# Four moves in a fused forward and backward transformer block: loads of x, constants, a layer norm's transposes, output gradients

## The chip, the cores and the metric

The kernel runs on one core of a Trainium2 chip. The metric is the device time of one execution in microseconds (us), lower is better. Every time quoted is from the runs of the kernel before, or from its profile, which is one profiled execution.

The engines are TensorE (PE, with PEld for its weight loads), VectorE (DVE), ScalarE (ACT), GpSimd (POOL) and SyncE (SP). Each takes its instructions in order. SP, ACT and POOL also issue transfers.

## The reference

One block on x of 2048 rows by 512 columns in bf16, forward and backward:

```
h  = x + attention(layernorm(x)) @ wo      # 32 heads of 16, each row sees 8 earlier rows, 2 apart
h2 = h + gelu(layernorm(h) @ w1 + b1) @ w2 + b2          # w1: 512 x 1792, w2: 1792 x 512
outputs: h2, and the gradients of x, wqkv, wo, w1, b1, w2, b2 for a given grad_out
```

The layer norms have no weights. The backward pass needs the normalised rows, attention's coefficients, q, k, v and the gelu's derivative.

## The kernel before, in words

The 2048 rows are cut into four chunks of 512. A tile of a chunk has 128 partitions; row-major tiles (`xt`, `ln1`, `ht`, `ln2`) hold four groups of 128 rows, feature-major tiles (`ln1T`, `ln2T`, `qt`, `kt`, `vt`) hold the transposes.

**Phase 1** is attention forward. Per chunk c:

- `p1_ln(c)` loads x into `xt` (L350, on SP's queue), normalises it on DVE (L194 statistics, L195, L198 `ve`, L199 `rstd` as a power on POOL, L201 `nm`, L203 four `ln` instructions), stores the rows by POOL's queue (L179), and transposes them on PE (L187) with copies on ACT (L188).
- `p1_qk(c)` and `p1_v(c)` are the projections (L366 on PE, L368 copies on ACT); `to_tm_store` (L235 on PE, L238 on ACT, L240 on SP) writes v, k and q back to memory row by row, through three staging buffers `tmst`.
- `p1_dots(c)` makes the products of q with eight shifted k's: four DVE instructions `pr` of 128x4096 (L257) and 64 small matmuls (L261). `p1_sm1`, `p1_sm2` are the softmax: maxima on DVE (L406, L410, L414) between copies on ACT (L404, L408, L412), a row-shift matmul (L416), exponentials (L419), sums (L427), reciprocal (L431), `attn` (L437).
- `p1_o(c, sc)`, twice per chunk, gathers rows of v by an indirect transfer from POOL's queue into one of two buffers `R` (L249), multiplies on DVE (`prb`, L287, four instructions) and sums on PE (`ps_band`, L292); `ost` is copied on ACT (L450), stored by POOL's queue (`o_d`, L453) and transposed into `oT` (L304, L305).
- `p1_d(c)` multiplies by wo and adds x (L463, L464, copy `h` L465), normalises h, stores it and transposes it into `ln2T[c]`.

`p1_round(c)` calls these for several chunks at once. The functions give an order of work and its dependencies; a scheduler then orders each engine's instructions up to the start of phase 3, so that an instruction may stand well ahead of or behind its place in the text.

**Before phase 1** stand the constants: `ident` (made on POOL), `Pmat`, `S32`, `Sum4`, `nSum4`, `Sm`, `ind8`, `Emat` (on DVE, L110 to L128), `mk` and the gather's row numbers `rowi` (on POOL, L130 to L145), and a few constant fills.

**SP's loads** take eight completion counters in turn. Where a load would take one that is in use, it waits for the transfer that used it last. Before: the x of chunk 0, three pieces of wqkv, four small stores of zeros (L476), `b1b` (L477), `b2row` (L478), then the x of chunks 1, 2 and 3. `b1b`, `b2row` and these three x loads wait for the first five transfers.

**Phase 2** is the MLP, forward and backward: projections `ps_h` (L577), gelu on DVE and ACT, `ps_f` (L609), `ps_gg` (L622), `ps_gl` (L633), with transposed loads and stores on SP (L561, L714 to L718).

**Phase 3** is attention backward. Here the order is written out by hand: `slot(us)` is called after each large DVE step, runs the PE work that was put off by `later(n, ...)` for n slots, and fills up with matmuls of the weight gradients (`filler`). `p3_go(c)` puts off four steps for chunk c: `a` transposes gh into `ghT`, `b(0)` and `b(2)` make two 128x512 groups each of `got = gh @ wo^T` (`go_mm`: L642 four matmuls, L643 a copy on ACT), `t` transposes and stores got. The tile `ps_go` is in the two-buffer pool psY, as `ps_band` (L1015) of the bands is. `psL` is a pool of one buffer of two banks that holds `ps_ga`. For chunk 1 all four steps run in one slot; chunk 0 is done earlier by `p3_pre`.

Of the kernel before, what the change touches and what calls it, by code (L numbers as in the profile page):

```python
# [10 lines left out]
P = 128  # L11
# [6 lines left out]
DH = 16  # L18
# [13 lines left out]
def _sub(apobj, dims, off=0):  # L32
    return _ap(apobj, [apobj.ap[0]] + [list(d) for d in dims], off)
# [3 lines left out]
def kernel(  # L37
# [29 lines left out]
    CH = 512  # L67
# [42 lines left out]
    V.tensor_copy(out=_sub(Pmat[:], [[1, 8], [8, DH]]), in_=_sub(ident[:], [[DH, 8], [1, DH]]))  # L110
    S32 = const.tile([P, 32], BF16, name="S32")
    for j in range(4):
        V.tensor_copy(out=S32[32 * j:32 * j + 32, :], in_=ident[32 * j:32 * j + 32, 32 * j:32 * j + 32])
    Sum4 = const.tile([P, P], BF16, name="Sum4")
    V.tensor_copy(out=Sum4[:].rearrange("p (a b) -> p a b", a=4), in_=S32[:].unsqueeze(1).to_broadcast([P, 4, 32]))
    nSum4 = const.tile([P, P], BF16, name="nSum4")
    V.tensor_scalar(out=nSum4[:], in0=Sum4[:], scalar1=-1.0, scalar2=None, op0=ALU.mult)
    Sm = const.tile([P, 4, P], BF16, name="Sm")
    V.memset(Sm[:], 0.0)
    for j in range(4):  # L120
        V.tensor_copy(out=Sm[32 * j:32 * j + 32, j, :], in_=Sum4[32 * j:32 * j + 32, :])
    ind8 = const.tile([P, 8], BF16, name="ind8")
    with nc.allow_low_precision(reason="exact 0/1 sums"):
        V.tensor_reduce(out=ind8[:], in_=ident[:].rearrange("p (a b) -> p a b", b=DH), axis=mybir.AxisListType.X, op=ALU.add)
    Emat = const.tile([P, 4, 32], BF16, name="Emat")
    V.memset(Emat[:], 0.0)
    for g in range(4):
        V.tensor_copy(out=Emat[:, g, 8 * g:8 * g + 8], in_=ind8[:])  # L128
    mk = const.tile([16, 2, 4, 32], BF16, name="mk")
    G.memset(mk[:], 0.0)  # L130
    for hf in range(2):
        G.affine_select(out=mk[:, hf], in_=mk[:, hf], compare_op=ALU.is_ge, fill=NEG, base=-2 * hf,
                        pattern=[[-4, 4], [0, 32]], channel_multiplier=1)
    ones_row = const.tile([1, P], BF16, name="ones_row")
    V.memset(ones_row[:], 1.0)
    ones_col = const.tile([P, 1], BF16, name="ones_col")
    V.memset(ones_col[:], 1.0)
    mhalf = const.tile([P, TPC], F32, name="mhalf")
    V.memset(mhalf[:], -0.5)
    zrow = const.tile([18, D], BF16, name="zrow")  # L140
    V.memset(zrow[:], 0.0)
    rowi = const.tile([P, 2], mybir.dt.uint32, name="rowi")
    for w4 in range(4):
        for b_, o in ((0, 4 * w4), (1, 4 * (3 - w4))):
            G.iota(rowi[32 * w4:32 * w4 + 32, b_:b_ + 1], pattern=[[0, 1]], base=o * D, channel_multiplier=8 * D)  # L145
# [201 lines left out]
    def p1_ln(c):  # L347
        xp, xg = ((wff, "w20"), (wff, "w28"), (early, "xt"), (late, "xt"))[c]
        xt = xp.tile([P, TPC, D], BF16, name="xt", tag=xg, bufs=1)
        load_rows(xt, xf, c)  # L350
        if c == 0:
            for i in range(3):
                o = (1, 0, 2)[i] * D
                SY.dma_start(out=wqkv[:, :, o:o + D], in_=A_wqkv[:, o:o + D].rearrange("(a p) j -> p a j", p=P))
        ln1 = early.tile([P, TPC, D], BF16, name="ln1", tag="ln1", bufs=2)
        layernorm(early, xt, rstd1, c, ln1)
        store_rows(ln1_d, c, ln1)
        ln1T = early.tile([P, DC, CH], BF16, name="ln1T", tag="ln1T", bufs=2)
        to_fm(ln1, ln1T)
        st_[c].update(xt=xt, ln1T=ln1T)  # L360
# [95 lines left out]
    def p1_d(c):  # L456
        d = st_[c]
        oT, xt = d["oT"], d["xt"]
        ht = htile(f"h{c}")
        for j in range(TPC):  # L460
            ps = X("ps_wo")
            for k in range(DC):
                T.matmul(ps[:], lhsT=oT[:, k, j * P:(j + 1) * P], rhs=wo[:, k, :], start=(k == 0), stop=False)  # L463
            T.matmul(ps[:], lhsT=ident[:], rhs=xt[:, j, :], start=False, stop=True)  # L464
            A.copy(out=ht[:, j, :], in_=ps[:])  # L465
        h_all.append(ht)
        ln2 = late.tile([P, TPC, D], BF16, name="ln2", tag="ln2", bufs=1)
        layernorm(late, ht, rstd2, c, ln2)
        store_rows(ln2_d, c, ln2)
        to_fm(ln2, ln2T[c])  # L470

    p1_ln(0)
    p1_qk(0)
    p1_dots(0)
    for (d_t, r) in ((v_d[0], 0), (k_d[0], 0), (q_d[NC - 1], CH), (go_d[NC - 1], CH)):
        SY.dma_start(out=d_t[r:r + RPAD, :], in_=zrow[:])  # L476
    SY.dma_start(out=b1b[:], in_=B_b1.rearrange("(f p) -> f p", p=P))  # L477
    SY.dma_start(out=b2row[:], in_=B_b2.rearrange("(a n) -> a n", a=1))  # L478
    G.dma_start(out=wo[:], in_=A_wo.rearrange("(a p) j -> p a j", p=P))
    p1_ln(1)  # L480
    p1_v(0)
# [6 lines left out]
    def p1_round(c):  # L488
        if c + 2 < NC:
            p1_ln(c + 2)  # L490
        if c + 1 < NC:
            p1_dots(c + 1)
        if c > 0:
            p1_d(c - 1)
        if c == NC - 2:
            p1_v(c + 1)
        if c + 2 < NC:
# [98 lines left out]
    def p2_rest(c):  # L596
# [33 lines left out]
        for j in range(TPC):  # L630
# [5 lines left out]
            ln_bwd(ffp["B"], ps[:], ln2[:, j, :], rstd2[:, t:t + 1], gout[:, j, :], gh[:, j, :])  # L636
            yield

    def go_mm(g, ghT, got):
# [3 lines left out]
        A.copy(out=got[:, g, :], in_=ps[:])  # L643
# [57 lines left out]
    p1_o(NC - 1, 1)  # L701
    run(hn, 1)
    p1_d(NC - 1)
    late.release()
    ffp["B"] = LP("ffB", "right")
    for k in range(SA, NS):
# [321 lines left out]
    def p3_go(c, at=(1, 2, 3, 4)):  # L1028
        ghT = pt3("ghT")
        got = pt3("got")  # L1030
        st3[c]["got"] = got

        def a():
            to_fm(gh_all[c], ghT)

        def b(g0):
            def f():
                for g in range(g0, g0 + 2):
                    go_mm(g, ghT, got)
# [185 lines left out]
```

## Time and profile before

| | us |
|---|---|
| median of 14 runs | 680.89 |
| lowest and highest run | 673.22 and 687.92 |
| the profiled execution's own time | 679.42 |
| its span in the profile | 677.5 |
| PE, DVE, ACT, POOL busy | 616.9, 512.9, 368.8, 150.2 |
| mean granted PE clock | 0.982 |

The profile's timeline gives start, duration, engine, line, output <- input, count, and in brackets how long the engine sat idle just before and what ended that. A chain of waits names who waited, for whom, how long in total, how often and the longest. A busy share is a mean over stages with different limits: PE is busy 80.32 of the first 100 us, 65.97 of the next 80, and 57.87 of the 60 after that.

### The profile page before, as it was taken

The numbers are of one execution on the slowest core, as the hardware profiler recorded it, in microseconds if no ns is written. First come the engines' busy times: TensorE is split into PE (matmuls) and PEld (weight loads), VectorE is DVE, ScalarE is ACT, GpSimd is POOL, SyncE is SP. The second block draws the span as 40 slices with busy tenths as digits, with TensorE's granted clock in tenths as the row PEclk, the third lists the DMA queues.
The fourth block names the chain that finished last, engine by engine and source line by source line (L and its number), as shares of the span: only waits on it lengthen the run. The fifth ranks groups of instructions, "written<-read, shape, count | busy, mean of one in ns | idle before, by whom it ended". The sixth has DMA issues, their size and how long they took to land. (4 is left out here: it accounts for less than half of the span.)

```text
span 677.5 us, 10267 instructions
## 1 busy us (share of the span) xinstructions
PE 616.9 (91%) x3948; PEld 289.4 (43%) x3948; DVE 512.9 (76%) x758; ACT 368.8 (54%) x576; POOL 150.2 (22%) x183
## 2 busy tenths in 40 slices
PE   3799998787999999999999898899989999988997
PEld 1343443333444344444344433434456576433443
DVE  6789989689779869869839697877977898296400
ACT  1497887699583555645440542763485357363311
POOL 4141635423001110110100251210322124030100
PEclk9999999988899999999999998999989999999999
DMA  7482959635999978978977899774898589969141
GB/s 256 153 293 88 299 191 306 209 133 125 231 208 282 245 199 193 233 226 186 228 236 186 288 349 379 263 272 171 289 402 309 189 278 340 326 236 317 62 155 47
DMA packets 147806, 158.87 MB, mean 235 GB/s; under 512 B 94461, under 2 KB 132398, under 8 KB 141102
## 3 DMA queue, kind: packets, MB, share of 16 engines
q1 hardware_dynamic: 120078, 69.58, 39.7%
q0 software_dynamic: 15376, 77.63, 32.8%
q10 hardware_dynamic: 12304, 11.01, 5.1%
q8 instruction: 31, 0.51, 0.3%
q14 instruction: 17, 0.14, 0.1%
HBM read 87.63 MB, written 48.03 MB: 200 GB/s over the span
## 5 line engine op out<-in xcount | busy, mean ns | idle before, releaser
L1007 DVE TENSOR_TENSOR prb<-R,cf 128x2048 bf16<-128x2048 bf16 x96 | 111.4, 1219 | 12.4 <-PE ps_band L1015 6.7
L209 ACT ACTIVATE gyr<-ps_gl,rstd 128x512 bf16<-128x512 f32 x32 | 21.9, 687 | 77.9 <-PE ps_gl L1071 32.0
L577 PE MATMUL ps_h<-ln2T,w 128*128 128x512 bf16 x224 | 58.2, 392 | 1.8 <-ACT xa L579 0.8
L891 PE MATMUL ps_gw<-gout_r,gwm 128*128 128x512 bf16 x224 | 55.4, 393 | 2.8 <-DMA gwm<-gT_d 2.8
L899 PE MATMUL ps_gw<-gwm,ln_r 128*128 128x256 bf16 x448 | 53.7, 275 | 2.3 <-DMA gwm<-ghT_d 1.6
L622 PE MATMUL ps_gg<-goT,w2T 128*128 128x512 bf16 x224 | 54.6, 378 | 0.3 <-DVE gb1p L624 0.3
L633 PE MATMUL ps_gl<-w1T,dt 128*128 128x512 bf16 x224 | 52.3, 379 | 1.6 <-ACT gyr L209 1.3
L609 PE MATMUL ps_f<-w,gt 128*128 128x512 bf16 x224 | 51.5, 379 | 0.7 <-DVE gt L585 0.7
L899 PEld LDWEIGHTS <-ln_r 128*128 128x128 bf16 x448 | 42.8, 98 | 14.1 <-issue 6.1
L646 DVE TENSOR_TENSOR pr<-got,vw 128x4096 bf16<-128x4096 bf16 x16 | 36.3, 2289 | 16.5 <-ACT got L643 11.2
L366 PE MATMUL ps_qkv<-ln1T,wqkv 128*128 128x512 bf16 x192 | 47.5, 393 | 1.0 <-ACT ln1T L188 0.6
L578 ACT ACTIVATE xb<-ps_h,b1c 128x512 bf16<-128x512 f32 x56 | 38.6, 697 | 16.3 <-DVE xa L589 10.7
L624 DVE CUSTOM_DVE_ANT_0 dt<-ps_gg,dt 128x512 bf16<-128x512 f32 x56 | 37.7, 685 | 11.2 <-PE ps_gg L622 11.2
L919 PE MATMUL ps_gwq<-gqh,ln_r 128*128 128x512 bf16 x192 | 42.6, 379 | 1.1 <-ACT gwst L818 1.1
L579 ACT ACTIVATE xa<-ps_h,b1c 128x512 bf16<-128x512 f32 x56 | 38.7, 702 | 7.0 <-DVE dt L590 7.0
L287 DVE TENSOR_TENSOR prb<-R,cf 128x2048 bf16<-128x2048 bf16 x32 | 37.6, 1206 | 5.2 <-DMA R<-v_d,rowi 5.2
L562 POOL DMA_DIRECT2D gT_d<-tst x16 | 12.0, 748 | 125.3 <-DMA tst<-gt 123.1
L1017 ACT ACTIVATE gks<-ps_band 128x512 bf16<-128x512 f32 x32 | 19.0, 598 | 36.3 <-PE ps_band L1015 31.3
L1015 PE MATMUL ps_band<-prb,S 128*32 128x512 bf16 x384 | 30.5, 385 | 8.7 <-ACT got L643 5.1
L238 ACT COPY tmst<-ptm 128x1024 bf16<-128x1024 bf16 x32 | 31.3, 1016 | 12.9 <-PE ptm L235 6.8
L257 DVE TENSOR_TENSOR pr<-qt,kt 128x4096 bf16<-128x4096 bf16 x16 | 36.0, 2284 | 1.2 <-PE ps_band L292 1.2
L577 PEld LDWEIGHTS <-w 128*128 128x128 bf16 x224 | 21.9, 100 | 29.2 <-issue 7.3
(183 smaller groups left out, 1128.9 us busy)
## 6 DMA issues: line engine op xcount, KB each, us to landing
gwm<-ghT_d SPq DMA_DIRECT2D x7, 1024.0 KB
gT_d<-tst POOLq DMA_DIRECT2D x12, 512.0 KB, 4.9
ghT_d<-tst POOLq DMA_DIRECT2D x12, 512.0 KB, 5.3
gwm<-gT_d SPq DMA_DIRECT2D x6, 1024.0 KB
out_dram<-gwst ACTq DMA_DIRECT2D x22, 256.0 KB
ln_d<-ln POOLq DMA_DIRECT2D x8, 512.0 KB, 4.4
vw<-vf_d SPq DMA_DIRECT2D x4, 528.0 KB
xt<-in_A_x_dram SPq DMA_DIRECT2D x4, 512.0 KB
```

The source lines that it names most:

```text
L366: T.matmul(ps[:], lhsT=wqkv[:, dc, sel * D + g * P:sel * D + (g + 1) * P], rhs=st_[c]["ln1T"][:, dc, :], start=(dc == 0), stop=(dc == DC - 1))
L577: T.matmul(ps[:], lhsT=wcol(w1, dc, f), rhs=ln2T[c][:, dc, :], start=(dc == 0), stop=(dc == DC - 1))
L578: A.activation(out=xb[:, f - f0, :], in_=ps[:], func=ACT.Identity, bias=b1c[:, f:f + 1])
L579: A.activation(out=x2[:, f - f0, :], in_=ps[:], func=ACT.Square, bias=b1c[:, f:f + 1])
L609: T.matmul(ps[:], lhsT=gts[f // 4][:, f % 4, j * P:(j + 1) * P], rhs=wrow(w2, f), start=(f == 0), stop=False)
L622: T.matmul(ps[:], lhsT=wcol(w2T, dc, f), rhs=goT[:, dc, :], start=(dc == 0), stop=(dc == DC - 1))
L624: V.tensor_tensor_reduce(out=dsl, in0=ps[:], in1=dsl, scale=1.0, scalar=0.0, op0=ALU.mult, op1=ALU.add, accum_out=gb1p[:, f, c:c + 1])
L633: T.matmul(ps[:], lhsT=dts[f // 4][:, f % 4, j * P:(j + 1) * P], rhs=wrow(w1T, f), start=(f == 0), stop=(f == FT - 1))
L891: yield from mm_pair("ps_gw2", lambda ps, o, u, i, t, k: T.matmul(ps[:], lhsT=g_[:, o, i * HN + t, :], rhs=gout_r[i][:, t, :], **k), MM, w ...
L899: yield from mm_pair("ps_gw1", lambda ps, o, u, i, t, k: T.matmul(ps[:, 256 * u:256 * u + 256].rearrange("p (a f) -> p a f", a=2), lhsT=ln ...
L919: yield from mm_pair("ps_gwq", lambda ps, o, u, i, t, k: T.matmul(ps[:], lhsT=ln1_r[i][:, t, (2 * d2 + o) * P:(2 * d2 + o + 1) * P], rhs=h ...
L1007: V.tensor_tensor(out=pr[:, 4 * hf:4 * hf + 4].rearrange("p j (d h) -> p j d h", h=H), in0=R[:, o:o + 4, :].rearrange("p j (d h) -> p j d ...
```

## The change

Four edits, in one kernel:

1. The four stores of zeros, `b1b` and `b2row` move from behind `p1_dots(0)` to the first `p1_round`, behind `p1_ln(2)`. In SP's queue the x of chunks 1 and 2 now stand right behind wqkv, then the six small transfers, then the x of chunk 3.
2. The constants that the first normalisation doesn't need (`Pmat`, `S32`, `Sum4`, `nSum4`, `Sm`, `ind8`, `Emat`, `mk`, `ones_col`, `rowi`) are made behind `p1_ln(0)`; `ident` and three fills stay in front.
3. `p1_d` ends with the stores of ln2. Its transposes are a function `p1_d2`, called behind `p1_v(c + 1)` in the last rounds and ahead of `p1_qk(c + 2)`.
4. In `p3_go`, `go_pair` makes two groups in one two-bank tile of `psL` and copies both at once.

```
-    V.tensor_copy(out=_sub(Pmat[:], [[1, 8], [8, DH]]), in_=_sub(ident[:], [[DH, 8], [1, DH]]))
...
     V.memset(ones_row[:], 1.0)
...
     V.memset(mhalf[:], -0.5)
...
     V.memset(zrow[:], 0.0)
...
-        to_fm(ln2, ln2T[c])
+        d["ln2"] = ln2
+
+    def p1_d2(c):
+        to_fm(st_[c]["ln2"], ln2T[c])

     p1_ln(0)
+    V.tensor_copy(out=_sub(Pmat[:], [[1, 8], [8, DH]]), in_=_sub(ident[:], [[DH, 8], [1, DH]]))
...
     p1_qk(0)
     p1_dots(0)
-    for (d_t, r) in ((v_d[0], 0), (k_d[0], 0), (q_d[NC - 1], CH), (go_d[NC - 1], CH)):
-        SY.dma_start(out=d_t[r:r + RPAD, :], in_=zrow[:])
-    SY.dma_start(out=b1b[:], in_=B_b1.rearrange("(f p) -> f p", p=P))
-    SY.dma_start(out=b2row[:], in_=B_b2.rearrange("(a n) -> a n", a=1))
...
     def p1_round(c):
         if c + 2 < NC:
             p1_ln(c + 2)
+        if c == 0:
+            for (d_t, r) in ((v_d[0], 0), (k_d[0], 0), (q_d[NC - 1], CH), (go_d[NC - 1], CH)):
+                SY.dma_start(out=d_t[r:r + RPAD, :], in_=zrow[:])
+            SY.dma_start(out=b1b[:], in_=B_b1.rearrange("(f p) -> f p", p=P))
+            SY.dma_start(out=b2row[:], in_=B_b2.rearrange("(a n) -> a n", a=1))
         if c + 1 < NC:
             p1_dots(c + 1)
         if c > 0:
             p1_d(c - 1)
         if c == NC - 2:
             p1_v(c + 1)
+        if c > 0:
+            p1_d2(c - 1)
         if c + 2 < NC:
             p1_qk(c + 2)
...
+    def go_pair(g0, ghT, got):
+        ps = psL.tile([P, 2, 512], F32, name="ps_go2", tag="l")
+        for g in range(g0, g0 + 2):
+            for dc in range(DC):
+                T.matmul(ps[:, g - g0, :], lhsT=wT["woT"][:, dc, g * P:(g + 1) * P], rhs=ghT[:, dc, :], start=(dc == 0), stop=(dc == DC - 1))
+        A.copy(out=got[:, g0:g0 + 2, :], in_=ps[:])
...
     p1_d(NC - 1)
+    p1_d2(NC - 1)
...
         def b(g0):
             def f():
-                for g in range(g0, g0 + 2):
-                    go_mm(g, ghT, got)
+                go_pair(g0, ghT, got)
             return f
```

The two programs differ in order beyond the text. On each engine the scheduler gave some of phase 1 another place; from the middle of phase 2's first chunk to phase 3 the order is the same.

More of the change, by code (lines that the diff above doesn't have):

```diff
@@ L109 @@
     Pmat = const.tile([P, P], BF16, name="Pmat")
-    V.tensor_copy(out=_sub(Pmat[:], [[1, 8], [8, DH]]), in_=_sub(ident[:], [[DH, 8], [1, DH]]))
     S32 = const.tile([P, 32], BF16, name="S32")
-    for j in range(4):
-        V.tensor_copy(out=S32[32 * j:32 * j + 32, :], in_=ident[32 * j:32 * j + 32, 32 * j:32 * j + 32])
     Sum4 = const.tile([P, P], BF16, name="Sum4")
-    V.tensor_copy(out=Sum4[:].rearrange("p (a b) -> p a b", a=4), in_=S32[:].unsqueeze(1).to_broadcast([P, 4, 32]))
     nSum4 = const.tile([P, P], BF16, name="nSum4")
-    V.tensor_scalar(out=nSum4[:], in0=Sum4[:], scalar1=-1.0, scalar2=None, op0=ALU.mult)
     Sm = const.tile([P, 4, P], BF16, name="Sm")
-    V.memset(Sm[:], 0.0)
-    for j in range(4):
-        V.tensor_copy(out=Sm[32 * j:32 * j + 32, j, :], in_=Sum4[32 * j:32 * j + 32, :])
     ind8 = const.tile([P, 8], BF16, name="ind8")
-    with nc.allow_low_precision(reason="exact 0/1 sums"):
-        V.tensor_reduce(out=ind8[:], in_=ident[:].rearrange("p (a b) -> p a b", b=DH), axis=mybir.AxisListType.X, op=ALU.add)
     Emat = const.tile([P, 4, 32], BF16, name="Emat")
-    V.memset(Emat[:], 0.0)
-    for g in range(4):
-        V.tensor_copy(out=Emat[:, g, 8 * g:8 * g + 8], in_=ind8[:])
     mk = const.tile([16, 2, 4, 32], BF16, name="mk")
[L130 to L133, printed above, removed]
     ones_row = const.tile([1, P], BF16, name="ones_row")
+    ones_col = const.tile([P, 1], BF16, name="ones_col")
+    mhalf = const.tile([P, TPC], F32, name="mhalf")
+    zrow = const.tile([18, D], BF16, name="zrow")
+    rowi = const.tile([P, 2], mybir.dt.uint32, name="rowi")
     V.memset(ones_row[:], 1.0)
-    ones_col = const.tile([P, 1], BF16, name="ones_col")
-    V.memset(ones_col[:], 1.0)
-    mhalf = const.tile([P, TPC], F32, name="mhalf")
     V.memset(mhalf[:], -0.5)
-    zrow = const.tile([18, D], BF16, name="zrow")
     V.memset(zrow[:], 0.0)
[L142 to L145, printed above, removed]
     rstd1 = const.tile([P, NT], F32, name="rstd1")
@@ L469, in p1_d, with p1_d2 @@
         store_rows(ln2_d, c, ln2)
-        to_fm(ln2, ln2T[c])
+        d["ln2"] = ln2
+    def p1_d2(c):
+        to_fm(st_[c]["ln2"], ln2T[c])
     p1_ln(0)
+    V.tensor_copy(out=_sub(Pmat[:], [[1, 8], [8, DH]]), in_=_sub(ident[:], [[DH, 8], [1, DH]]))
+    for j in range(4):
+        V.tensor_copy(out=S32[32 * j:32 * j + 32, :], in_=ident[32 * j:32 * j + 32, 32 * j:32 * j + 32])
+    V.tensor_copy(out=Sum4[:].rearrange("p (a b) -> p a b", a=4), in_=S32[:].unsqueeze(1).to_broadcast([P, 4, 32]))
+    V.tensor_scalar(out=nSum4[:], in0=Sum4[:], scalar1=-1.0, scalar2=None, op0=ALU.mult)
+    V.memset(Sm[:], 0.0)
+    for j in range(4):
+        V.tensor_copy(out=Sm[32 * j:32 * j + 32, j, :], in_=Sum4[32 * j:32 * j + 32, :])
+    with nc.allow_low_precision(reason="exact 0/1 sums"):
+        V.tensor_reduce(out=ind8[:], in_=ident[:].rearrange("p (a b) -> p a b", b=DH), axis=mybir.AxisListType.X, op=ALU.add)
+    V.memset(Emat[:], 0.0)
+    for g in range(4):
+        V.tensor_copy(out=Emat[:, g, 8 * g:8 * g + 8], in_=ind8[:])
+    G.memset(mk[:], 0.0)
+    for hf in range(2):
+        G.affine_select(out=mk[:, hf], in_=mk[:, hf], compare_op=ALU.is_ge, fill=NEG, base=-2 * hf,
+                        pattern=[[-4, 4], [0, 32]], channel_multiplier=1)
+    V.memset(ones_col[:], 1.0)
+    for w4 in range(4):
+        for b_, o in ((0, 4 * w4), (1, 4 * (3 - w4))):
+            G.iota(rowi[32 * w4:32 * w4 + 32, b_:b_ + 1], pattern=[[0, 1]], base=o * D, channel_multiplier=8 * D)
     p1_qk(0)
     p1_dots(0)
[L475 to L478, printed above, removed]
     G.dma_start(out=wo[:], in_=A_wo.rearrange("(a p) j -> p a j", p=P))
@@ L490, in p1_round @@
             p1_ln(c + 2)
+        if c == 0:
+            for (d_t, r) in ((v_d[0], 0), (k_d[0], 0), (q_d[NC - 1], CH), (go_d[NC - 1], CH)):
+                SY.dma_start(out=d_t[r:r + RPAD, :], in_=zrow[:])
+            SY.dma_start(out=b1b[:], in_=B_b1.rearrange("(f p) -> f p", p=P))
+            SY.dma_start(out=b2row[:], in_=B_b2.rearrange("(a n) -> a n", a=1))
         if c + 1 < NC:
@@ L496, in p1_round @@
             p1_v(c + 1)
+        if c > 0:
+            p1_d2(c - 1)
         if c + 2 < NC:
@@ L637, in p2_rest, with go_pair @@
             yield
+    def go_pair(g0, ghT, got):
+        ps = psL.tile([P, 2, 512], F32, name="ps_go2", tag="l")
+        for g in range(g0, g0 + 2):
+            for dc in range(DC):
+                T.matmul(ps[:, g - g0, :], lhsT=wT["woT"][:, dc, g * P:(g + 1) * P], rhs=ghT[:, dc, :], start=(dc == 0), stop=(dc == DC - 1))
+        A.copy(out=got[:, g0:g0 + 2, :], in_=ps[:])
     def go_mm(g, ghT, got):
@@ L703 @@
     p1_d(NC - 1)
+    p1_d2(NC - 1)
     late.release()
@@ L1037, in f @@
             def f():
-                for g in range(g0, g0 + 2):
-                    go_mm(g, ghT, got)
+                go_pair(g0, ghT, got)
             return f
```

## The prediction

> **What bounds the kernel now.** I read the busy shares by stage first. From 180 us to the end PE is the bound; before that no engine is, and PE loses 33.7 of 180 us. Its waits there are therefore the stage to read, and what they hang on is mostly DVE (85.17 of the first 100 us busy). The first fence is the windows' answer (last columns: granted clock, transfer share, GB/s).
>
> ```profile
> 0.00:100.00 100.00, 80.32 (x637) 37.78 (x641) 85.17 (x148) 66.86 (x103) 35.49 (x54) 1.00 0.65 215
> 100.00:180.00 80.00, 65.97 (x432) 29.21 (x427) 67.19 (x97) 60.50 (x84) 28.76 (x34) 0.91 0.69 195
> 180.00:240.00 60.00, 57.87 (x258) 24.25 (x257) 50.56 (x91) 36.38 (x59) 6.30 (x8) 1.00 1.11 248
> ```
>
> Next, the waits of DVE and SP up to 180 us, and of PE behind 175 us: two large waits for transfers, SP's x loads held by wqkv, and one wait of bands for `got`.
>
> ```profile
> DVE st L194 <- DMA xt<-in_A_x_dram: 9.0, 3, 6.3
> DVE prb L287 <- DMA R<-v_d,rowi: 5.2, 1, 5.2
> SPq L176 <- DMA wqkv<-in_A_wqkv_dram: 3.5, 2, 2.5
> PE ps_band L1015 <- ACT got L643: 5.1, 4, 2.1
> ```
>
> Last, the timeline around these places.
>
> ```profile
> 8.52 2.36 SPq L176 DMA_DIRECT2D xt<-in_A_x_dram  x3
> 21.07 0.69 DVE L194 BATCH_NORM_STATS2 st<-xt 128x6 f32<-128x512 bf16 x1 [6.25 <-DMA xt<-in_A_x_dram]
> 22.35 4.48 DVE L257 TENSOR_TENSOR pr<-qt,kt 128x4096 bf16<-128x4096 bf16 x2
> ...
> 120.09 1.86 SPq L240 DMA_DIRECT2D v_d<-tmst  x2
> 122.83 2.14 POOL L453 DMA_DIRECT2D o_d<-ost  x4 [5.68 <-ACT ost L450]
> 125.28 1.66 POOL L249 DMA_INDIRECT R<-v_d,rowi  x1 [0.30 <-issue]
> 134.03 1.22 DVE L287 TENSOR_TENSOR prb<-R,cf 128x2048 bf16<-128x2048 bf16 x1 [5.21 <-DMA R<-v_d,rowi]
> ...
> 437.08 0.61 PE L1015 MATMUL ps_band<-prb,S 128*32 128x512 bf16 x8 [2.09 <-ACT got L643]
> ```
>
> DVE takes its work in order, and the scheduler put a statistic of chunk 2's x (21.07) ahead of `ve` of chunk 1 and of the four products `pr`. So the third x load holds up everything, though the first q and k copies end at 18.2. At 134.03 the gather for chunk 3 is late, because POOL's queue holds it behind four `o_d` stores that wait for `ost`.
>
> **Part 1 and 2: the start.** Now x of chunks 1 and 2 is issued right behind wqkv, at about 2.9, not 8.52. Six tiles of 0.524 MB make 3.15 MB. The windows move 0.11 MB to 2.5 us, then 363, 294 and 191 GB/s in steps of 2.5 us, the last with SP held. At 294 GB/s from 7.5 on, all has landed at 12.2; at 191, at 14.8. DVE, below, asks for the third x at 15.9, so this wait goes at either end. The six small transfers and x of chunk 3 go behind; the program makes that last load wait for chunk 1's x, and DVE needs it only at about 29.5.
>
> [...]
>
> DVE's chain: `ve` of chunk 0 at 7.17 and the power (1.04) stay, so `nm` at 8.58. Then two of the S32 copies (0.43) and the four `ln` (1.64): they end at 10.8 against 11.71, and PE's projections start 0.9 earlier than 13.58. The other constants (0.43, 0.28, 0.18, 0.35, 0.16, 0.19, 1.01, overlapping by some 0.4) end at 13.0; they now follow where the wait for x was, so this costs nothing; without it, 2.2. Statistics of chunk 1 as in 11.91 to 14.82, 2.9: 15.9. Three statistics and `ve` of chunk 2's round, 2.2, `nm`: 18.2. Two products 4.48: 22.7 (their second q copy, 19.96 before, is 0.9 earlier). Three `ln` 1.06, two products 4.49, one `ln` 0.4: 28.6. Before, the same stood at 32.75: 4.1 earlier.
>
> Up to `attn` of chunk 0 (48.05) the order now holds all of chunk 3's normalisation too (statistics and four `ln`, 1.38 of which stood at 69.50). The span 32.75 to 48.05 takes 15.3; with 1.38 more and POOL's power waited for twice (0.5 and 0.8 for 0.55 before), less the 0.85 that fills the 1.74 us wait at `attn`, it is 16.4: `attn` at 45.0, 3.05 earlier, and 1.4 more is saved at 69.5.
>
> **Part 3: a wait that is added.** In round 1 the 16 transposes of ln2 of chunk 0 now stand on PE ahead of the last four of the 32 projections; before, they stood among the bands. Aligned at the reciprocal of chunk 1 (65.48 before), PE reaches them at 84.7: products end at 76.0, then eight sums and nine wo matmuls to 78.5, then 28 x 0.22. DVE's four `ln` stand behind two `prb`, `m3` and a third `prb`, and start at 85.95; the first two are done at 86.6. PE waits 1.6 to 1.9. Queued behind it: the last q copy, the row-shift matmul L416, both bands; behind those, on ACT, two ln2T copies (1.93) ahead of that q copy and the exponentials (1.0). I follow them to the reciprocal at 95.27: bands end at 90.1 as before, exponentials at 91.1 against 88.5, the sums behind v's transposes at 95.6. So the reciprocal of chunk 2 is 0.4 late in this frame, and the 1.4 of the `ln` moved out is gone. Net of parts 1 to 3 at that point: 3.05 - 0.4 = 2.6. Ends: if PE waited until the `ln` end of before (88.55), 3.9, the term would be 0.3; with no wait, 4.4.
>
> PE's rate after a gap is the unknown there. The projections at 13.96 to 17.38 show weight loads 0.43 apart, the next 21 take 4.49 (0.21 each): a slow start of about 4 us behind the idle first 10 us. [...] I take no such cost.
>
> **The gather of chunk 3.** p1_d2 changes the order here. ACT's two `tmst` copies of v now precede the ln2T copies: PE transposes v once m3 is there (113.7 in before's time, since m3 too moves ahead of a `prb`), the copies end at 116.4 instead of 121.5, and SP issues the v stores at 115.6 and 116.5 instead of 120.09. POOL's queue now holds the gather ahead of the `o_d` stores; its buffer comes free with the fourth `prb`, at 119.1. The gather starts between 119.6 and 121.3 (a store-to-gather step took at most 4.3, 36.16 to 40.48), and took 8.75 (125.28 to 134.03): 128.4 to 130.1. DVE gets there at 128.6. Of 5.21 some 1.5 may stay. The eight `o_d` stores behind the gather lose about 1 and nobody waits for them; the second gather starts near 129.5 instead of 130.81, so it is late next, by 0.6 to 1.9, partly shared with the sigmoid's table load (1.28). ACT's wait for `k_d` (4.6 at 135.51), which held h of chunk 2, ends as the gather's traffic does, earlier too. I take 4.3; ends 0 and 5.4. Behind 143 DVE is the limit up to PE's start of ps_f at 175.31, and SP's transposes start when gelu's first block ends (153.86), so both move with it.
>
> **Part 4: pairs.** The 5.1 us of bands waiting for `got` (0.69, 2.09, 0.22, 2.09) end, since `ps_go` no longer takes the bands' buffers. But at 437.08 the band's `prb` ends only at 435.1 (it started at 432.76), and the next band's `prb` waits for `cf` and that for `sh` on ACT (436.45), which hardly moves. I count 0.3 for each wait of 2.09 and 0.4 for the first: 1.0. Pair 2 needs pair 1's copy (one buffer; 1024 wide 1.0); a band and eight transposes (0.61 + 0.55) cover that. For chunk 1 nothing covers it: 1.3, and the last copy is 0.4 longer: 1.7, of which PE's next waits for `prb` (0.29 and 0.73) take 1.0. Net 1.0 - 0.7 = 0.3; ends -1.7 (no gain, nothing absorbed) and 3.4.
>
> **Sum:** 2.6 + 4.3 + 0.3 = 7.2. The profiled execution took 679.42, 1.47 under the median of the runs: 672.2 in its terms, **673.7** for the median. The ends together give 682.3 and 667.7 (-1.4 and 13.2). A difference of 0.5% (3.4 us: 677.5 and 684.3) is about what a measurement can tell from no change.
>
> **Rivals.**
>
> 1. The gather is not earlier. For: stores can land slowly, those of k issued at 126.93 kept ACT until 135.51, 8.6 later; v's at 116.5 would then land at 125.1, where the gather started anyway. Against: no gather runs at that time. Only 2.9 stays: **678.0**.
> 2. The start is lost. PE waits 3.9 in round 1, DVE stands in line behind the bands, and 0.3 of the start is left, with the gather's gain: 4.9, **676.0**. Against: DVE's sums above put the `ln` 1.6 behind PE, not 3.9.
> 3. Slower: the granted clock. It was 0.91 in 100 to 180 us and 1.00 in 180 to 240. PE is the bound from 175 on, so 0.91 there costs 5.4 per 60 us. From 80 us of it the 7.2 are eaten; from 118 us the kernel is 0.5% slower; with 150 us it stands at **687**. For: runs of before spread from 673.22 to 687.92. Against: the low clock stands where PE has gaps (0.91 also at 400 to 420, PE 17.21 of 20), and the change closes gaps.
>
> **How the numbers follow.** Forecast 0.64 (its own range 668 to 677.4), rival 1 0.18 (675 to 681), rival 2 0.10, rival 3 0.08. Faster: nearly all of the first (0.62), a third of rival 1 (0.06), most of rival 2 (0.07): 0.75. Same 0.17, slower 0.08. The range 667.5 to 680.5 takes in the upper end of the sum's terms and rival 1's place, and leaves out rival 3 and some of each edge.
>
> **What would show it.** Right: no wait of DVE for x behind 5 us; the four products end near 28; `attn` of chunk 0 near 45; a wait of PE L187 for `ln` of 1.6 to 1.9 near 82; the gather of chunk 3 issued ahead of `o_d`, and DVE's wait for it under 2; ps_f starting near 168; no wait of L1015 for `got`, and about 1.3 of PE's second pair for the first copy near 376. Wrong: the reciprocal of chunk 2 later than 93.5, ps_f behind 172, or a clock under 0.97 behind 175.

## The result, and the profile after

| | before | changed |
|---|---|---|
| median (runs) | 678.09 (47) | 666.35 (10) |
| lowest and highest run | 672.89 and 687.92 | 664.22 and 672.45 |
| ratio of the runs, with its 95% interval | | 0.9845 [0.9815, 0.9876] |
| profiled execution, its span | 679.42, 677.5 | 667.02, 665.1 |
| PE busy, mean granted clock | 616.9, 0.982 | 610.2, 0.990 |

(Times in us. Ratios, here and below, leave out the runs over 1.5% above the fastest of their kernel, so they are not exactly the quotient of the medians.) The forecast was 673.7 with a range of 667.5 to 680.5: the direction was right, and the time fell 1.2 below the range. Two later comparisons of the same kernel with before (a2 and a3 below) gave 669.37 at 0.9871 [0.9815, 0.9927] and 667.89 at 0.9899 [0.9855, 0.9943]. The three ratios average 0.987, a gain of 8.7 us.

The same windows as before, in the changed kernel (busy time of PE, weight loads, DVE, ACT, POOL; then granted clock, transfer share, GB/s):

```profile
0.00:100.00 100.00, 80.40 (x629) 37.24 (x630) 86.42 (x147) 66.45 (x102) 37.09 (x53) 0.98 0.65 214
100.00:180.00 80.00, 67.02 (x453) 29.70 (x451) 70.48 (x101) 61.32 (x86) 28.71 (x34) 0.94 0.73 205
180.00:240.00 60.00, 57.29 (x255) 24.11 (x254) 50.59 (x90) 36.16 (x59) 7.60 (x10) 1.00 1.10 249
400.00:420.00 20.00, 19.97 (x150) 8.23 (x149) 15.56 (x14) 7.11 (x11) 7.78 (x8) 1.00 0.94 353
```

Up to 240 us the busy shares hardly moved. The last line is the surprise: this stretch was at clock 0.91 with PE busy 17.21 before, and the forecast expects no gain there. The waits of the changed kernel, which answer to those shown of before:

```profile
DVE st L173 <- DMA xt<-in_A_x_dram: 2.5, 1, 2.5
DVE prb L266 <- DMA R<-v_d,rowi: 1.6, 1, 1.6
PE ptm L214 <- ACT got L650: 3.2, 3, 1.1
PE ps_go L649 <- ACT got L650: 1.1, 1, 1.1
```

The wait for x shrank from 9.0 to the first one's 2.5, that for the gather from 5.2 to 1.6, and no band waits for `got` any more; the transposes `ptm` and one second pair wait instead. SP's wait for wqkv moved from the x loads (3.5) to `b1b` and `b2row` (1.4 and 1.2). Line numbers of early lines are lower by 21 (L194 is now L173), late ones higher by 14 (L1015 is L1029). The timeline at the places that the forecast spoke of:

```profile
2.88 1.55 SPq L155 DMA_DIRECT2D xt<-in_A_x_dram  x2
18.41 4.49 DVE L236 TENSOR_TENSOR pr<-qt,kt 128x4096 bf16<-128x4096 bf16 x2
86.77 0.28 PE L166 MATMUL pt<-ident,ln 128*128 128x128 bf16 x2 [1.30 <-DVE ln L182]
121.81 1.11 POOL L228 DMA_INDIRECT R<-v_d,rowi  x1 [3.64 <-DVE prb L266]
122.92 2.18 POOL L432 DMA_DIRECT2D o_d<-ost  x4
129.62 1.22 DVE L266 TENSOR_TENSOR prb<-R,cf 128x2048 bf16<-128x2048 bf16 x1 [1.55 <-DMA R<-v_d,rowi]
427.77 0.61 PE L1029 MATMUL ps_band<-prb,S 128*32 128x512 bf16 x8
```

Each step looks as it was forecast: the x loads at 2.88, the products 4 us earlier, the gather ahead of the stores, the band without a wait. What they were worth is another matter. Followed by the same place in both traces, the gain is 4.2 behind the four products and the `ln` among them (32.75 and 28.6), -0.3 at the reciprocal of chunk 2 (95.27 and 95.55), 3.7 at ps_f (175.31 and 171.60), 2.3 at the first `ps_go` of chunk 1 (381.71 and 379.42), and 12.4 at the kernel's last transpose, `pgb` (645.13 and 632.75). Ten of the twelve come from phase 3, where the forecast had 0.3.

### The profile page after: what moved, and what is told of

The parts are those of the page before. It is cut to its first block, busy times and chain, and to the rows that moved or that the text cites. A ratio compares the mean times of both kernels' runs of the same rounds, so it can differ in the third digit from the quotient of the medians.

```text
span 665.1 us, 10258 instructions
## 1 busy us (share of the span) xinstructions
PE 610.2 (92%) x3948; PEld 285.2 (43%) x3948; DVE 514.0 (77%) x758; ACT 367.2 (55%) x570; POOL 155.3 (23%) x183
## 5 line engine op out<-in xcount | busy, mean ns | idle before, releaser
L583 PE MATMUL ps_h<-ln2T,w 128*128 128x512 bf16 x224 | 55.8, 379 | 0.8 <-ACT xa L585 0.4
L905 PE MATMUL ps_gw<-gout_r,gwm 128*128 128x512 bf16 x224 | 52.7, 380 | 0.0
L345 PE MATMUL ps_qkv<-ln1T,wqkv 128*128 128x512 bf16 x192 | 48.1, 394 | 0.7 <-DMA go_d<-zrow 0.6
L590 ACT ACTIVATE xa<-xa 128x2048 bf16<-128x2048 bf16 (+1 forms) x16 | 27.1, 1700 | 13.6 <-DVE xa L589 13.6
L639 PEld LDWEIGHTS <-dt 128*128 128x128 bf16 x224 | 21.4, 98 | 30.2 <-issue 3.0
```

The costliest lines, as they stand in the source:

```text
L345: T.matmul(ps[:], lhsT=wqkv[:, dc, sel * D + g * P:sel * D + (g + 1) * P], rhs=st_[c]["ln1T"][:, dc, :], start=(dc == 0), stop=(dc == DC - 1))
L583: T.matmul(ps[:], lhsT=wcol(w1, dc, f), rhs=ln2T[c][:, dc, :], start=(dc == 0), stop=(dc == DC - 1))
L639: T.matmul(ps[:], lhsT=dts[f // 4][:, f % 4, j * P:(j + 1) * P], rhs=wrow(w1T, f), start=(f == 0), stop=(f == FT - 1))
L905: yield from mm_pair("ps_gw2", lambda ps, o, u, i, t, k: T.matmul(ps[:], lhsT=g_[:, o, i * HN + t, :], rhs=gout_r[i][:, t, :], **k), MM, w ...
```

## The experiments

All labels are used in the table at the end of this section, which has one row for each profile.

**Which edits.** Four kernels on one chip: edit 4 alone, all but edit 4, edits 1 and 2 alone, edit 3 alone.

```
e1: before, with         go_pair(g0, ghT, got)            in b(g0)
e2: changed, with        for g in range(g0, g0 + 2): go_mm(g, ghT, got)
e3: e2, with             to_fm(ln2, ln2T[c])              at the end of p1_d again
e4: before, with         p1_d2 as in edit 3
```

> The kernel before with edit 4 alone (go_pair). Theory A (the shortfall of the forecast is the pairs): the two traces part by 2.3 us up to phase 3 and by 10 more between 400 and 440 us, so the pairs alone bring 8 to 10 us, and 20 us behind the first pairs the granted clock is 1.00 instead of 0.91 to 0.97; PE's wait of 2.8 for the transposed loads gwm and the half-rate matmuls behind it are gone. Theory B (the pairs are worth the 0.3 of the forecast, and 400 to 440 us differed because everything ahead of it came at another time): within 1.5 us of before, gwm wait and low clock still there. Theory C (the gwm wait is the mood of one execution): about 4 us, the band waits of 5.1 gone, the gwm wait there or not.

> The changed kernel with edit 4 undone (edits 1 to 3 stay). Theory A: only 2 to 3 us faster than before, with waits of the bands for got near 5 us in all and a granted clock under 0.98 between 390 and 440 us. Theory B: 9 to 10 us faster than before, as the changed kernel. Theory C: 5 to 7 us faster.

> The kernel before with edits 1 and 2 alone (loads of x, constants). The forecast reckoned these without the wait that edit 3 adds in round 1: the third product ends 4.1 us earlier, attn of chunk 0 2 to 3 us earlier, and the reciprocal of chunk 2 up to 4.4 us earlier, as no PE wait for ln2 stands in front; gather of chunk 3 not earlier than the start moved, so DVE waits near 5 us for it again. Theory A1 (edit 3's wait in round 1 ate the start): reciprocal of chunk 2 at 91.5 to 93.5, end 2 to 4 us earlier. Theory A2 (the start was lost to something else, before round 1 or behind it): reciprocal of chunk 2 at 94.5 to 95.5, end within 1.5 us of before.

> The kernel before with edit 3 alone (the transposes of ln2 as a function of their own). It should issue the gather of chunk 3 ahead of the stores of o_d and take DVE's wait for it from 5.2 to under 2. Theory A1: PE waits about 1.5 or more for ln2 in round 1 and the reciprocal of chunk 2 comes 0.5 to 2 us later than in before (95.27), so the end gains only 0 to 3 us of the 4.4. Theory A2: reciprocal of chunk 2 within 0.5 us of before and the whole gather gain of 3.7 us stays to ps_f, and 2 us of it to the end.

Measured: e1 670.05, ratio 0.9864 [0.9805, 0.9924]; e2 675.22, 0.9966 [0.9927, 1.0005]; e3 676.97, 0.9983 [0.9943, 1.0024]; e4 674.71, 0.9957 [0.9903, 1.0012]; before 679.3 in 29 runs. The pairs alone bring nearly everything, and edits 1 to 3 together 2.3 us with zero just inside the interval. Theory A holds for the total and fails for its detail: the wait for gwm was still there in e1 (2.95), so its absence in the changed kernel's profile needed another explanation.

The same chunk of the bands in e2 and in e3, both without pairs, shows what a wait of 2.09 costs (timeline of PE; first e2, then e3):

```profile
434.08 0.61 PE L1029 MATMUL ps_band<-prb,S 128*32 128x512 bf16 x8 [2.09 <-ACT got L656]
434.63 1.89 PE L905 MATMUL ps_gw<-gout_r,gwm 128*128 128x512 bf16 x4
436.31 1.86 PE L214 MATMUL ptm<-Pmat,got 128*128 128x128 bf16 x16
```

```profile
435.75 0.62 PE L1023 MATMUL ps_band<-prb,S 128*32 128x512 bf16 x8 [2.09 <-ACT got L651]
436.30 1.04 PE L899 MATMUL ps_gw<-gout_r,gwm 128*128 128x512 bf16 x4
437.17 1.06 PE L214 MATMUL ptm<-Pmat,got 128*128 128x128 bf16 x16
```

The wait is equal. Behind it, e2's four matmuls take 1.89 and its transposes 1.86, e3's take 1.04 and 1.06: in e2 PE runs at half rate for some 3.5 us, and loses 1.6. The seven profiles without pairs have two such waits each (chunks 2 and 3); 11 of the 14 were followed by the half rate. What tells the two apart is shown below, in b2.

e3 has the PE order of round 1 that the forecast put down to edit 3, though edit 3 is absent (timeline of PE in e3; L345 are the last projections):

```profile
77.31 6.45 PE L345 MATMUL ps_qkv<-ln1T,wqkv 128*128 128x512 bf16 x28
85.05 0.28 PE L166 MATMUL pt<-ident,ln 128*128 128x128 bf16 x2 [1.30 <-DVE ln L182]
85.18 0.38 PE L345 MATMUL ps_qkv<-ln1T,wqkv 128*128 128x512 bf16 x1
```

e4, which has edit 3, has neither the order nor the wait. The scheduler turned that order because of the other edits.

**The tile or the copy, and the rest of the sum.**

```
e5: changed, with        for g in range(g0, g0 + 2): A.copy(out=got[:, g, :], in_=ps[:, g - g0, :])
e7: before, with edits 3 and 4
e8: e7, with each load of gwm from gT_d as two of 0.5 MB:
        for a_ in range(2):
            SY.dma_start(out=t_[:, a_]..., in_=src[:, 2 * q + a_]...)
a2: the changed kernel again
```

> The changed kernel as it is, for a second profile. The first profile lacked PE's wait for the transposed loads gwm near 407 us (2.1 to 3.0 in the five other profiles, with ten matmuls at 0.40 behind it); there the second gather of go took 8.92 to issue and the gathers of k came 7.7 later, so the load had less company. If that was the mood of one execution, the wait of 2 to 3 is here again and the profile is some 4 longer than the first. If the four edits together remove it, it is absent again. The time stays 1.2 to 1.8% under before either way.

> The changed kernel, the pair of groups in one two-bank tile of psL as in edit 4, but copied by two copies of 512 each instead of one of 1024. Theory D1 (what counts is that ps_go left the bands' two buffers): same as the changed kernel within 1 us, no wait of the bands for got. Theory D2 (the single copy counts): 2 us or more over the changed kernel. The copies together take 1.3 to 1.4 against 1.0, so the second pair of a chunk waits some 0.4 longer where nothing covers it, once, in chunk 1.

> The kernel before with edits 3 and 4, without 1 and 2. In round 1 the trace of e3 has the transposes of ln2 ahead of the last projections and a PE wait of 1.30 though edit 3 was absent, and e4 has neither. Theory E1 (edits 1 and 2 turn the order of round 1 and lose there what they gain at the start): as fast as the changed kernel or up to 2 us faster, the DVE wait for x at 4 to 9 us, reciprocal of chunk 2 no later than 95 less what x came earlier. Theory E2 (edits 1 and 2 bring their start): 2 to 4 us slower than the changed kernel.

> As e7_d2_and_pairs, and each load of the transposed g (gwm, 1 MB) issued as two of 0.5 MB, of which the first 16 matmuls need only the first. Theory F1 (the wait of 2 to 3 near 405 us is the load's landing, and it halves the rate of ten matmuls behind it): no PE wait for gwm, ten matmuls at 0.21, granted clock 1.00 from 400 to 420, and 4 to 4.5 us faster than e7 in the profile; 2 to 4.5 in the medians, as not every execution need have the wait. Theory F2 (both halves land together, or the wait goes elsewhere): within 1 us of e7.

Measured: a2 669.37, 0.9871 [0.9815, 0.9927]; e5 667.04, 0.9839 [0.9787, 0.9890]; e7 670.19, 0.9877 [0.9821, 0.9934]; e8 669.67, 0.9855 [0.9797, 0.9913]. D1 holds: with two copies it is as fast as with one, so it is the own tile that counts. e7, without edits 1 and 2, is as fast as a2 within the intervals (E1). a2 had the wait for gwm again (2.5), with slow matmuls behind it. e8 told nothing on the load, since e7 and e8 both had no such wait.

**The wait for gwm.** The load has two buffers; it is issued when the older one is free (396.14 in e2) and is needed some 9 us later. Whether it lands in time goes with how the gathers ahead of it are issued. POOL's gathers of go, DVE's four products `pr`, then PE, in e2:

```profile
393.46 2.74 POOL L228 DMA_INDIRECT R<-go_d,rowi  x1 [14.92 <-ACT gwst L832]
396.50 1.89 POOL L228 DMA_INDIRECT R<-go_d,rowi  x1 [0.30 <-issue]
393.10 8.89 DVE L659 TENSOR_TENSOR pr<-got,vw 128x4096 bf16<-128x4096 bf16 x4
407.10 4.02 PE L905 MATMUL ps_gw<-gout_r,gwm 128*128 128x512 bf16 x10 [2.12 <-DMA gwm<-gT_d]
```

and in the changed kernel's first profile, where the wait is missing:

```profile
393.19 8.92 POOL L228 DMA_INDIRECT R<-go_d,rowi  x1 [14.70 <-ACT sh L1064]
402.42 0.94 POOL L228 DMA_INDIRECT R<-go_d,rowi  x1 [0.30 <-issue]
392.40 8.89 DVE L659 TENSOR_TENSOR pr<-got,vw 128x4096 bf16<-128x4096 bf16 x4
404.70 2.76 PE L905 MATMUL ps_gw<-gout_r,gwm 128*128 128x512 bf16 x12
```

With the short issue, both gathers and then those of k (399.90) run beside the load, and PE waits 2.12, then takes 0.40 for a matmul instead of 0.23. With the long one (8.92) they come later, and the load is in time.

The rows of DVE show where the issue ends. In all twenty profiles the longer issue ends 0.81 to 0.82 after the end of one of the four products (2.28 each, one right behind the other): the first in eleven profiles (2.74 in e2), the fourth in nine (402.11 against 401.29 here). So by these rows the issue waits for DVE's products, for one of them or for all four. Where the first of the two gathers starts does not decide which: 0.0 to 1.0 behind the start of the first product in the eleven, 0.8 to 1.4 in the nine.

To see whether the load is what PE waits for, and whether pairs decide the mode:

```
e9:  before,  with the split load of e8
e10: changed, with the split load of e8
b2:  before again          e1_again: e1 again
```

> The kernel before with each 1 MB load of the transposed g (gwm) issued as two of 0.5 MB, and no other edit. The four profiles without edit 4 all show PE's wait of 2.1 to 3.0 for this load near 407 us and ten matmuls at 0.32 to 0.40 instead of 0.21 behind it. Theory F1 (the wait is the landing of the load's last bytes and costs the wait and the slow matmuls): no PE wait for gwm or under 0.5, granted clock 1.00 from 400 to 420, and 3.5 to 4.5 us under before. Theory F2 (the halves land together because the gathers of k hold the transfer engines): the wait stays over 1.5 and the time is within 2 us of before.

> The changed kernel with the split load of e9. If the wait is there in a third to a half of the changed kernel's executions (two of six profiles with edit 4 show it), the split brings 1 to 2 us in the median over the changed kernel and takes away its longer runs: 1.6 to 1.9% under before. If the wait has nothing to do with the load's size, as the changed kernel.

> The kernel before as it is, for a second profile. The three profiles with before's own order at the start show DVE waits for x of 9.0, 6.1 and 4.9; expected is one of 4.5 to 9.5 here, the wait of PE for gwm of 2 to 3 near 409 (if its lack belongs to the pairs and not to chance), a gather of go that is issued in under 3, the band waits of 5.1 and at least one half-rate stretch behind them.

> The kernel before with edit 4 alone, for a second profile. Band waits for got gone, from ps_go of chunk 2 to the end about 5 us less than in a profile without pairs that has the half-rate stretches, 3 less than in one that has none. If pairs shift the gathers of go for good, the long issue of a gather (8.5 to 8.9) is here and the wait for gwm is not; the first profile of this kernel had it the other way round, so half and half is expected.

Measured: e9 675.43, 0.9950 [0.9911, 0.9990], its wait 0.27 and the matmuls behind it at full rate, with the short issue: F1, a little under the 3.5 to 4.5 expected. e10 668.39, 0.9843 [0.9799, 0.9887]: as the changed kernel, and its wait was still 1.15. b2 675.12 (one run): short issue, wait 2.4, but no half rate behind it. e1_again 676.78 (one run): long issue (8.94), and a wait of 0.3.

b2 also shows which waits the half rate follows. Its band waits in chunks 2 and 3 are both 2.09 (ending at 434.48 and 499.52), and only the first is followed by it (windows of PE: length, busy time, granted clock, transfer share, GB/s):

```profile
431.16:434.58 3.42, 1.33 (x10) 1.00 0.89 343
434.58:437.99 3.41, 3.41 (x21) 0.50 0.14 58
496.02:499.43 3.41, 1.41 (x7) 1.00 1.07 428
499.43:502.85 3.42, 3.33 (x44) 1.00 0.98 390
```

In every profile the stretches of clock 0.50 last 3.41 or two or three times that (but for one that the kernel's end cuts off), and they start on one grid of steps of 3.41, which lies elsewhere in each profile (in before at 116.92, 137.40, 154.47, 171.54, 410.47, 437.78 and 502.63; in the changed kernel's first profile at 24.48 and 130.29, and at 150.77 for 6.83). The windows above are such steps. The first wait lies whole in one step, and the next step is at clock 0.50. Of the second, 2.00 lies in one step and 0.09 in the next, and the clock stays at 1.00. The same holds for all 23 waits of the bands and of gwm of 2.0 to 3.0: in the 18 that were followed by the half rate, one step holds 2.09 to 3.02 of the wait, in the five others at most 2.00.

**The start, and the mode once more.**

```
h3:  e10, with p1_d2(0) called behind p1_sm2(2) instead of ahead of p1_qk(3)
f2:  changed, with the four zero stores, b1b and b2row back behind p1_dots(0)   (edits 2, 3, 4)
b3:  before again          e1c: e1 again
```

> The changed kernel with the split load of e9, and in round 1 the transposes of ln2 of chunk 0 called behind p1_sm2(2), so that on PE they stand among the second bands and the wo matmuls, not ahead of the last four projections. Theory A (that place is where the start's gain is lost): no PE wait of 1.3 for ln near 86, the reciprocal of chunk 2 starts 1.5 to 3 earlier than the 93.8 to 95.6 of the profiles with edits 1 and 2, so at 91 to 93, ps_f 1 to 3 earlier, and the median 1 to 3 us under the changed kernel: 1.7 to 2.2% under before. Theory B (ACT or DVE are just as late, and PE's wait only shows it): reciprocal of chunk 2 within 0.7 of those, no gain in the median.

> The changed kernel with edit 1 undone: constants behind the first normalisation, transposes of ln2 apart and pairs stay, the six small transfers go back ahead of the x of chunks 1 to 3. Theory A: the wait for x is 6 to 11 (the earlier start only lengthens it), the PE order of round 1 is that of before with no wait for ln, reciprocal of chunk 2 at 92 to 97, and the median within 2 us of the changed kernel. Theory B (the early loads carry part of the gain): 2 to 4 us slower than the changed kernel.

> The kernel before, third profile. If pairs decide how the gather of go is issued: under 3 again, and PE waits 2 to 3 for gwm. If it is chance (four in eleven): a third for the long issue, with no wait.

> Edit 4 alone, third profile. If pairs decide: the long issue in two of three, and then no wait for gwm. Band waits for got gone in any case, and from ps_go of chunk 2 to the end some 3 to 5 us less than in the third profile of before.

Measured: h3 670.13, 0.9885 [0.9832, 0.9939]; f2 667.90, 0.9809 [0.9752, 0.9866]; b3 681.66 and e1c 670.82 (one run each). h3 has no wait for `ln` in round 1, and its reciprocal of chunk 2 is at 92.57, 1.3 to 3.1 ahead of the seven profiles with the turned order; but ps_f is at 174.23, later than the 172.1 that six of these average (all but e3, which lacks edit 3), and the median gains nothing. So the place of the transposes costs the start 1.6 (from the reciprocal of chunk 1 to that of chunk 2 takes 31.2 in all seven and 29.6 in h3), and putting it right only moves the loss behind 100 us.

f2 went against both theories. Its loads of x stand behind the six small transfers as in before (8.92), yet DVE waits for no x but the first (timeline of DVE):

```profile
14.96 1.27 DVE L173 BATCH_NORM_STATS2 st<-xt 128x6 f32<-128x512 bf16 x2
16.37 4.49 DVE L236 TENSOR_TENSOR pr<-qt,kt 128x4096 bf16<-128x4096 bf16 x2
```

With the constants late and the loads late, the scheduler put the products ahead of chunk 2's statistics. They start 2.0 earlier than in the changed kernel, and no early load is needed. Its order of round 1 is that of before, too: it is edit 1, on top of edit 2, that turns it (edit 1 alone was not run).

**Is edit 1 a loss?** The last two kernels shared a chip:

```
i1: f2, with the split load of e8          a3: the changed kernel again
```

> Edits 2, 3 and 4 with the split load of e9, without edit 1. If edit 1 costs what the traces say (first products 2.4 earlier without it, reciprocal of chunk 2 at 92.3 against 93.8 to 95.6): 2 us or more under the changed kernel on the same chip, 1.8 to 2.3% under before; no wait of DVE for x but the first of 2.6, and no PE wait for gwm over 1.2. If the start is given back behind 100 us whatever its order: within 1 us of the changed kernel.

> The changed kernel again, beside i1: 1.2 to 1.8% under before; x wait 2.5, PE wait for ln of 1.3 near 86, the long or the short issue of the gather of go, and with the short one a wait for gwm of 2 to 3.

Measured: i1 666.55, 0.9874 [0.9802, 0.9947]; a3 667.89, 0.9899 [0.9855, 0.9943]. i1's reciprocal of chunk 2 is at 91.90 against 95.63, but its median is only 1.3 lower, well inside the intervals. No version was shown to beat the changed kernel. Edit 1 is worth nothing that these runs can tell.

All profiles, in us: DVE's wait for x; start of the second eight sums `ps_L` (first products done); reciprocal of chunk 2; ps_f; from the first `ps_go` of chunk 1 to the last transposes ("phase 3"); the longer issue of a gather of go; PE's wait for gwm.

| profile | edits | x | sums | recip. | ps_f | phase 3 | gather | gwm |
|---|---|---|---|---|---|---|---|---|
| before | none | 9.0 | 26.9 | 95.27 | 175.3 | 263.4 | 2.6 | 2.8 |
| b2 | none | 8.0 | 25.9 | 94.23 | 175.1 | 259.3 | 2.6 | 2.4 |
| b3 | none | 11.7 | 29.6 | 100.37 | 181.2 | 259.7 | 2.4 | 2.0 |
| e9 | split | 7.6 | 25.5 | 93.98 | 174.2 | 259.2 | 2.1 | 0.3 |
| e3 | 1 2 | 2.6 | 22.7 | 93.83 | 174.4 | 258.7 | 2.1 | 2.5 |
| e4 | 3 | 4.9 | 22.8 | 91.23 | 169.5 | 262.6 | 2.6 | 3.0 |
| e2 | 1 2 3 | 2.6 | 23.1 | 94.22 | 171.5 | 262.0 | 2.7 | 2.1 |
| e1 | 4 | 6.1 | 23.9 | 92.28 | 172.1 | 258.5 | 1.9 | 3.0 |
| e1_again | 4 | 9.1 | 27.0 | 97.05 | 177.4 | 253.8 | 8.9 | 0.3 |
| e1c | 4 | 8.1 | 26.0 | 94.47 | 172.4 | 253.5 | 8.9 | 0 |
| e7 | 3 4 | 9.4 | 27.3 | 98.27 | 175.7 | 252.5 | 8.9 | 0 |
| e8 | 3 4 split | 8.2 | 26.1 | 94.58 | 175.5 | 254.0 | 8.5 | 0 |
| f2 | 2 3 4 | 2.6 | 20.6 | 92.34 | 171.4 | 257.3 | 2.8 | 2.6 |
| i1 | 2 3 4 split | 2.5 | 20.3 | 91.90 | 171.4 | 254.1 | 8.3 | 0 |
| changed | 1 2 3 4 | 2.5 | 23.0 | 95.55 | 171.6 | 253.3 | 8.9 | 0 |
| a2 | 1 2 3 4 | 2.5 | 22.9 | 94.07 | 171.8 | 257.2 | 2.7 | 2.5 |
| a3 | 1 2 3 4 | 2.5 | 23.0 | 95.63 | 174.4 | 252.5 | 8.4 | 0 |
| e5 | 1 2 3 4, two copies | 2.6 | 23.1 | 94.20 | 170.1 | 253.0 | 8.5 | 0 |
| e10 | 1 2 3 4 split | 2.6 | 23.0 | 94.17 | 172.9 | 254.7 | 2.3 | 1.2 |
| h3 | 1 2 3 4 split, order | 2.6 | 23.1 | 92.57 | 174.2 | 254.2 | 8.7 | 0 |

## Why the forecast was wrong, step by step

The sum was 2.6 + 4.3 + 0.3 = 7.2, and the gain is about 8.7. That nearness is an accident: all three terms were mis-sized, the first two too large and the third far too small. By the table, edits 1 to 3 bring 3.3 up to ps_f (175.4 on average in the seven profiles with neither edit 3 nor early loads, 172.1 in the six with edits 1, 2 and 3 and the order of the changed kernel), and pairs 6.3 in phase 3 (260.9 in six profiles without, 254.6 in nine with, split loads left out).

**The start, 2.6; measured 0.7.** (0.1 if b3, the latest of the ten profiles with the old start, is left out.) The first step was sized well, and three behind it failed.

- Up to `attn` of chunk 0 the forecast holds. The 9.0 of waits for x was one execution's, and the other nine profiles with the same loads and constants show 4.9 to 11.7; but on average the sums start at 23.0 instead of 26.1, 3.1 earlier, and `attn` at 44.9 instead of 47.9, 3.0 earlier, against 3.05 forecast.
- The 3.05 was carried over unchanged to the reciprocal of chunk 1. There 2.0 is left (63.3 instead of 65.3): DVE now waits 0.97 to 0.98 for the sums `ps_L` behind `attn` (first line below), in all seven and in none of the ten.
- From there to the reciprocal of chunk 2 the forecast had 0.4 more; it takes 31.2 in all seven and 29.8 to 30.1 in the ten, 1.4 more. The wait of PE for `ln` is not what was mis-sized: it is 1.30 (1.6 to 1.9 forecast) and costs 1.6 by h3, where the forecast's 4.4 and 2.6 differ by 1.8. What went uncounted is that DVE waits 0.94 for POOL's power at `nm` (second line below; before has no such wait there, h3 has it too) and 0.43 for `pb`; so of the 1.4 of the `ln` moved out little was saved. The order itself comes from edit 1 and not from edit 3 (e3 against e4; f2 against the changed kernel). The seven profiles have the reciprocal of chunk 2 at 94.5 on average, the ten at 95.2; the 0.3 that I gave as the lower end was the better value, and the mark "later than 93.5" was crossed in all seven. The changed kernel's first profile is at 95.55 and a3 at 95.63, 1.5 behind the other five, since in these two PE ran a step of 3.41 at half rate near 24 us, another cost of a kind that the forecast left out.
- That the early load is needed at all. f2 has no wait for x without it, as the order on DVE does the same.

The lines for this, from the changed kernel's first profile (the third belongs to the next paragraph):

```profile
47.58 2.29 DVE L236 TENSOR_TENSOR pr<-qt,kt 128x4096 bf16<-128x4096 bf16 x1 [0.98 <-PE ps_L L240]
85.09 0.16 DVE L180 SCALAR_TENSOR_TENSOR nm<-mv,rstd 128x4 f32<-128x4 f32 x1 [0.94 <-POOL rstd L178]
152.45 1.86 PE L442 MATMUL ps_wo<-wo,oT 128*128 128x512 bf16 x4 [4.00 <-ACT xa L585]
```

**The gather of chunk 3, 4.3; measured 1.9.** The mechanism is as forecast: issued at 121.81 ahead of `o_d` instead of 125.28, DVE's wait 1.55 instead of 5.21, its `prb` 4.4 earlier. In the changed kernel's first profile 4.0 of it was left at ps_f. Over the profiles, from the reciprocal of chunk 2 to ps_f takes 80.1 on average without edit 3 (eight) and 78.2 with it (eleven, h3 left out). What failed is "Behind 143 DVE is the limit": in the changed kernel DVE waits 2.8 there for `xa` on ACT, and PE 4.0 for `xa` at `ps_wo` (last line above). All twelve profiles with edit 3 have these two waits, of 2.8 to 4.1 and of 3.9 to 4.1; the eight without it have at most 0.8 of either. I had counted the sigmoid's load of its table with 1.28 inside "late next" and did not follow ACT's queue further.

**Pairs, 0.3; measured 6.3, and 0.9864 as a ratio for edit 4 alone.** Here lies the miss. It has three layers.

- Structure. I counted 0.3 for each band wait of 2.09, since the band's `prb` and the next one's `sh` hardly move. That is so: `cf` comes 0.4 earlier. But behind it e3's DVE waits 0.53 and 0.88 for late bands in chunk 2, and e1's only 0.43. Against e3, whose clock stays full there, the pairs save 1.5 in chunk 2 and 1.0 in chunk 3. Chunk 1 loses 0.4, where I had -0.7 net. Together 2.1, within my ends of -1.7 and 3.4.
- The half rate. "I take no such cost" is the step that failed; no row showed that a wait comes without it. A wait of 2.09 was followed by a step of 3.41 at half rate in 11 of 14 places; against e3 this costs 1.6 in chunk 2 and 1.1 to 1.3 in chunk 3. I had a row that spoke for the cost: rival 3 quotes clock 0.91 at 400 to 420, where PE had waited 2.79 for gwm, and uses it only to argue that low clock and gaps go together.
- The wait for gwm, which the forecast doesn't mention. It was missing in the profiles with the long issue of the go gather, and there phase 3 takes 253.1 (six profiles with pairs) against 257.7 with the short one (three): 4.6, the wait and its half rate. The long issue stood in none of seven profiles without pairs and in 9 of 13 with them. So the pairs bring it about more often than not. That the issue ends 0.81 to 0.82 behind one of DVE's products is shown above; why behind the first in some executions and behind the fourth in others, and what the pairs do to it, is open. The gather waits for the stores of go, and these come from copies of `got` that edit 4 shifts; whether that is the cause wasn't tried.

By chunk, from one first `ps_go` to the next and to the last transpose, the 6.3 are 1.8, 2.8 and 1.8 (46.3 to 44.5, 65.3 to 62.5, 149.4 to 147.6).

**Rivals.** Rival 2, the start lost, is what happened in the main, by several shorter waits and not by one of 3.9. Rival 1 did not: the gather is earlier. Rival 3, a lower clock, was the wrong way round: the clock was the largest unpriced gain.

## What to carry to other kernels

A wait of PE must be priced with what follows it: to take away a wait of 2.09 brought 1.5 and 1.0 here where the clock had stayed full, and 3.1 and 2.1 to 2.3 where it had not. A wait for a transfer in one profile is one draw (4.9 to 11.7 for the same loads here): before its length enters a sum, look whether a slower engine's order and not the transfer decides it. And where a scheduler orders the work, a gain at the start has to be followed to the first place where its order differs, as that is where it is given back.

## What was not expected of the hardware

- PE ran at half rate behind waits of 2.0 to 3.0 in 18 of 23 places (11 of 14 at the bands, 7 of 9 behind the wait for gwm, where ten matmuls took 3.2 to 4.0 instead of 2.33). b2's wait of 2.4 and b3's of 2.0 were not followed by it, e2's of 2.1 was: what tells the two apart in these 23 is whether 2.09 or more of the wait falls into one step of the 3.41 grid. It doesn't hold beyond them: at `ps_f` in e5 a step with 1.68 of a wait was enough.
- The longer issue of chunk 1's two indirect gathers of go takes 1.9 to 2.8 or 8.3 to 8.9, with nothing between in twenty profiles, and ends 0.81 to 0.82 behind the first of DVE's four products or behind the fourth; and the slow mode goes with the faster kernel, where the load beside it lands in time.
- From ps_f to the first `ps_go`, 171.3 to 173.2 in sixteen profiles, the four others took 176.0 to 176.9 (e1_again, e1c, e5, e10), for no edit that they share. In these four DVE waits 2.4 to 3.9 for a transposed transfer (`tst` from `dt`) between 224 and 233 us, PE behind it 2.6 to 4.1 for `gt` at `ps_f`, and a step at half rate follows; in the sixteen these waits are at most 1.4 and 1.6. Why the transfer lands late is open.
